# Issuing the first weight quarter from ScalarE's DMA queue instead of SyncE's

## The chip, the cores and the metric

The kernel runs on one core of one Trainium2 chip. The metric is the device time of one execution in microseconds (us); lower is better. Of the 46 executions of the kernel before, 45 lie within 0.3% of their mean (493.22 us), and the effect studied here is smaller than that, so I look at distributions and at the traces as well as at medians. A verdict of "faster" or "slower" needs 2%.

## The reference, cut to what matters

The program computes two attention blocks on the same input `x` (2048 rows of 1024) and mixes them with a gate. Only the very first stage matters here: the key projection of block A and the feature map applied to it.

```python
def _A_ref(x, wqkv, wo):
    qkv = (x @ wqkv).reshape(B, S, 3, H, Dh)...     # B=1, S=2048, D=1024, H=32
    q, k, v = qkv[0], qkv[1], qkv[2]
    phi = lambda t: jnp.where(t > 0, t + 1, jnp.exp(t)) + 1e-6
    pq, pk = phi(q), phi(k)
    ...
# then block B (sliding, dilated) and g * a + (1 - g) * b
```

## The kernel before

TensorE needs `x` transposed (`xT`) and the weights `WkA`. All loads are issued by SyncE, in program order, on one queue. `xT` comes in sixteen DMA transposes of 128 rows (256 KB each); the first half of `WkA` (512 columns) comes in four quarters of 256 KB; its second half is one 1 MB load behind the last transpose.

```python
nc.scalar.preload_act_table_set("natural_log_exp_and_others")
...
WkA = [wpool.tile([P, KT, 512], BF16, name="WkA0", tag="wa")]
nc.sync.dma_start_transpose(out=xT[:, :, 0:P], in_=rows(x, 0, P))
for i in range(4):
    if i == 2:
        nc.sync.dma_start_transpose(out=xT[:, :, P:2 * P], in_=rows(x, P, 2 * P))
    nc.sync.dma_start(out=WkA[0][:, 2 * i:2 * i + 2, :],
                      in_=A_wqkv[2 * i * P:(2 * i + 2) * P, D:D + 512].rearrange("(kt p) n -> p kt n", p=P))
for t in range(2, NB):
    nc.sync.dma_start_transpose(out=xT[:, :, t * P:(t + 1) * P], in_=rows(x, t * P, (t + 1) * P))
WkA += load_w("WkA", A_wqkv, D, "wa", only=(1,))
# ... then xrow (4 MB), WvA, WoA, WvB, WqA on the same queue
```

On TensorE, 36 small matmuls on constants come first (the warm-up), then the projection, first with the pieces of two row blocks interleaved in the order in which the loads arrive, then block by block:

```python
warm_up(36)                       # 128x128 matmuls of ones
for t, kts in ((0, (0, 1, 2, 3)), (1, (0, 1, 2, 3)), (0, (4, 5)), (1, (4, 5)), (0, (6, 7)), (1, (6, 7))):
    for kt in kts:
        project(first[t], t, kt, 0)          # quarter kt // 2 of the weights, row block t
    ...
for half in range(2):             # 16 row blocks with the first weight half, 16 with the second
    for t in range(NB):
        ...
# then G = xrow^T pk (line L202), which needs all 256 projections
```

## Time and profile before

| what | value | where it is read |
|---|---|---|
| time, median of the first 3 runs | 493.66 us (492.73 to 494.03) | the runs |
| span of the traced execution, PE busy in it | 491.1 us, 481.1 us | the page's first part |
| TensorE idle before its first real matmul | 0.68 us, until quarter one | the timeline |
| second transpose of `x` | issued 3.31, landed 7.6 us | the timeline and the line's own view |
| second weight half | issued 26.40, landed 34.87 us | the chain of waits |

The first part of the page of the kernel before gives each engine's busy time. TensorE, busy for 481.1 of 491.1 us, is the bottleneck of nearly the whole span.

```profile
PE 481.1 (98%) x3276; PEld 230.0 (47%) x3336; DVE 282.8 (58%) x548; ACT 180.6 (37%) x279; POOL 7.6 (2%) x26
```

The timeline of the kernel before, first 12 us. Columns: start, length, engine (SPq and ACTq are queue instructions, that is, the issuing of a DMA), source line, operation, destination and source, count, and in brackets the engine's idle time before and what ended it.

```profile
0.79 1.28 ACT L72 ACT_TABLE_LOAD   x1 [0.79 <-PEq L513]
0.80 1.34 SPq L97 DMA_TRANSPOSE xT<-in_A_x_dram  x1
...
1.11 4.02 PE L163 MATMUL warm<-onesb 128*128 128x128 bf16 x36 [1.11 <-DVE onesb L116]
...
2.19 1.07 SPq L101 DMA_DIRECT2D WkA_75<-in_A_wqkv_dram  x2
...
3.31 1.25 SPq L100 DMA_TRANSPOSE xT<-in_A_x_dram  x1
4.61 1.09 SPq L101 DMA_DIRECT2D WkA_75<-in_A_wqkv_dram  x2
...
5.81 1.42 PE L157 MATMUL pk_ps<-WkA_75,xT 128*128 128x512 bf16 x4 [0.68 <-DMA WkA_75<-in_A_wqkv_dram]
...
7.66 4.71 PE L157 MATMUL pk_ps<-WkA_75,xT 128*128 128x512 bf16 x20 [0.42 <-DMA xT<-in_A_x_dram]
```

SyncE needs 1.25 to 1.34 us to issue each of these two transposes and about 0.5 us to issue a quarter. TensorE waits twice, for quarter one and for the second transpose. The chain of waits of the kernel before, in the first 36 us (start, length, what), ends in SyncE's queue and the 1 MB load behind it:

```profile
25.05 1.31 SPq L104
26.35 0.04 issue
26.40 8.47 DMA WkA_96<-in_A_wqkv_dram
34.87 0.05 issue
34.92 1.25 PE pk_ps L157 x5
```

The windows view of the kernel before: window, length, busy time (count) of PE, weight loads, DVE, ACT and POOL, then clock, DMA share, GB/s. (A packet's whole time is counted in the window in which it starts, so a share can pass 1.)

```profile
1.50:2.00 0.50, 0.50 (x8) 0.50 (x6) 0.17 (x2) 0.50 (x1) 0.50 (x4) 1.00 0.00 0
2.00:2.50 0.50, 0.50 (x8) 0.50 (x6) 0.00 (x0) 0.07 (x1) 0.50 (x4) 1.00 0.09 22
2.50:3.00 0.50, 0.50 (x7) 0.50 (x6) 0.00 (x0) 0.00 (x0) 0.50 (x5) 1.00 0.99 232
3.00:3.50 0.50, 0.50 (x7) 0.50 (x6) 0.00 (x0) 0.00 (x0) 0.50 (x4) 1.00 1.17 248
3.50:4.00 0.50, 0.50 (x8) 0.50 (x6) 0.00 (x0) 0.00 (x0) 0.50 (x3) 1.00 0.85 94
4.00:4.50 0.50, 0.50 (x7) 0.50 (x6) 0.00 (x0) 0.00 (x0) 0.50 (x3) 1.00 0.72 190
```

### The profile page before, as it was taken

Reading aid. Unit: us, or ns where it says so; the run is one execution under the profiler, and the core shown is the slowest. Engines: PE = TensorE matmul, PEld = TensorE weight load, DVE = VectorE, ACT = ScalarE, POOL = GpSimd, SP = SyncE. Lnnn points to the kernel's source line nnn. Section 1 sums busy time; section 2 is a strip of 40 time slices with the busy share of each in tenths; the row PEclk is TensorE's granted clock in tenths of the full one; section 3 lists DMA queues with packets and bytes.
Section 4 is the critical chain, followed back from the end, with each engine's and each line's share of the span. In section 5 each row is a group of like instructions: output and inputs, shape, how many; then the busy total and the mean of one; then the engine's idle time right before and its main releaser. Section 6 shows DMA issues by size and latency. Waiting matters only on the chain.

```text
span 491.1 us, 8153 instructions
## 1 busy us (share of the span) xinstructions
PE 481.1 (98%) x3276; PEld 230.0 (47%) x3336; DVE 282.8 (58%) x548; ACT 180.6 (37%) x279; POOL 7.6 (2%) x26
## 2 busy tenths in 40 slices
PE   8999999999999999999999999999999999999997
PEld 5444444446444444444445444444544444444444
DVE  1666669951329999997476767676765496000000
ACT  2333321112543333332555555655565333112121
POOL 3000000000200000000000000000000000000000
PEclk9999999999999999999999999999999999999999
DMA  8999950001521222235011133111174933010101
GB/s 195 173 297 368 348 183 0 0 1 44 177 76 54 86 94 92 73 135 173 4 34 30 32 96 54 26 36 37 29 136 90 217 87 84 35 43 33 43 34 43
DMA packets 80309, 46.56 MB, mean 95 GB/s; under 512 B 53648, under 2 KB 74256, under 8 KB 80272
## 3 DMA queue, kind: packets, MB, share of 16 engines
q1 hardware_dynamic: 80272, 46.04, 34.4%
q8 instruction: 26, 0.43, 0.4%
q14 instruction: 11, 0.09, 0.1%
HBM read 21.23 MB, written 7.34 MB: 58 GB/s over the span
## 4 chain that ended last, share of the span: by engine, by line
PE 91%; SPq 5%; DMA 2%; issue 1%; DVE 0%; ACT 0%; ACTq 0%
PE kq_ps L338 23%; PE d_ps L457 21%; PE g_ps L202 11%; PE p_ps L261 11%; PE p_ps L295 8%; PE pk_ps L157 6%; SPq L104 4%; PE q_ps L295 2%; DMA WkA_96<-in_A_wqkv_dram 2%; PE kv_ps L220 1%; PE q_ps_4355 L457 1%; PE p_ps L250 1%; PE q_ps L457 1%; SPq L101 0%; PE q_ps_4236 L295 0%
## 5 line engine op out<-in xcount | busy, mean ns | idle before, releaser
L202 PE MATMUL g_ps<-pk,xrow 128*128 128x512 bf16 x251 | 55.2, 379 | 0.3
L145 DVE TENSOR_SCALAR e<-e 128x512 f32<-128x512 f32 x64 | 27.2, 425 | 42.7 <-ACT e L144 42.7
L462 ACT ACTIVATE osb<-d_ps,omg 128x512 bf16<-128x512 f32 (+1 forms) x31 | 20.9, 673 | 74.5 <-PE d_ps L457 68.7
L157 PEld LDWEIGHTS <-xT 128*128 128x128 bf16 x256 | 24.9, 98 | 32.5 <-issue 1.5
L457 PEld LDWEIGHTS <-OBT 128*128 128x128 bf16 x264 | 25.8, 98 | 29.2
L202 PEld LDWEIGHTS <-xrow 128*128 128x128 bf16 x256 | 25.0, 98 | 30.2
L261 PEld LDWEIGHTS <-xT 128*128 128x128 bf16 x256 | 25.0, 98 | 30.2
L295 PEld LDWEIGHTS <-xT 128*128 128x128 bf16 x256 | 24.2, 98 | 28.0
L144 ACT ACTIVATE e<-pk_ps 128x512 f32<-128x512 f32 x32 | 19.0, 597 | 42.3 <-PE pk_ps L157 33.2
L377 DVE TENSOR_TENSOR PT_1863<-PT_1863,mask 128x672 bf16<-128x672 bf16 (+3 forms) x42 | 23.7, 571 | 17.9 <-ACT PT_1863 L375 17.4
L338 PE MATMUL kq_ps<-xT,WqB_1846 128*128 128x512 bf16 x120 | 31.8, 379 | 1.0 <-issue 0.6
L338 PE MATMUL kq_ps<-xT,WqB_1844 128*128 128x512 bf16 x124 | 31.7, 379 | 0.7 <-issue 0.5
L377 DVE TENSOR_TENSOR PT_1864<-PT_1864,mask 128x672 bf16<-128x672 bf16 (+3 forms) x40 | 22.3, 565 | 17.0 <-ACT PT_1864 L375 16.5
L338 PE MATMUL kq_ps<-xT,WkB_1041 128*128 128x512 bf16 x122 | 31.6, 379 | 0.2
L344 DVE CAST kqt<-kq_ps 128x512 bf16<-128x512 f32 x32 | 22.0, 687 | 16.5 <-PE kq_ps L338 16.5
L338 PE MATMUL kq_ps<-xT,WkB_1039 128*128 128x512 bf16 x120 | 30.7, 379 | 0.4 <-issue 0.2
L261 PE MATMUL p_ps<-WvB_112,xT 128*128 128x512 bf16 x126 | 30.6, 379 | 0.1
L261 PE MATMUL p_ps<-WvB_110,xT 128*128 128x512 bf16 x125 | 30.6, 379 | 0.1
L266 ACT CAST tmp<-p_ps 128x512 bf16<-128x512 f32 x32 | 18.8, 588 | 30.2 <-PE p_ps L261 27.9
L457 PEld LDWEIGHTS <-pqT_4413 128*128 128x128 bf16 x200 | 19.6, 98 | 22.1
L157 PE MATMUL pk_ps<-WkA_75,xT 128*128 128x512 bf16 x125 | 28.1, 380 | 1.4 <-DMA WkA_75<-in_A_wqkv_dram 0.7
L457 PE MATMUL d_ps<-WoB_4050,OBT 128*128 128x512 bf16 (+1 forms) x126 | 28.3, 365 | 0.1
(393 smaller groups left out, 665.8 us busy)
## 6 DMA issues: line engine op xcount, KB each, us to landing
xrow<-in_A_x_dram SPq DMA_DIRECT2D x4, 1024.0 KB, 13.0
out_dram<-osb SPq DMA_DIRECT2D x31, 128.0 KB, 1.9
pqd<-tmp SPq DMA_DIRECT2D x12, 256.0 KB, 2.0
V<-tmp SPq DMA_DIRECT2D x4, 264.0 KB, 2.4
WkA_75<-in_A_wqkv_dram SPq DMA_DIRECT2D x4, 256.0 KB, 3.8
WkA_96<-in_A_wqkv_dram SPq DMA_DIRECT2D x1, 1024.0 KB, 8.5
WvA_102<-in_A_wqkv_dram SPq DMA_DIRECT2D x1, 1024.0 KB, 15.3
WvA_104<-in_A_wqkv_dram SPq DMA_DIRECT2D x1, 1024.0 KB, 14.7
```

The costliest lines, as they stand in the source:

```text
L104: nc.sync.dma_start_transpose(out=xT[:, :, t * P:(t + 1) * P], in_=rows(x, t * P, (t + 1) * P))
L144: nc.scalar.activation(out=e[:], in_=pj[:], func=ACT.Exp)
L145: nc.vector.tensor_scalar(out=e[:], in0=e[:], scalar1=1.0, scalar2=1e-6, op0=ALU.min, op1=ALU.add)
L157: nc.tensor.matmul(pj[:], lhsT=xT[:, kt, t * P:(t + 1) * P], rhs=WkA[half][:, kt, :], start=(kt == 0), stop=(kt == KT - 1))
L202: nc.tensor.matmul(pj[:], lhsT=xrow[:, t, kt * P:(kt + 1) * P], rhs=pk[:, t, half * 512:(half + 1) * 512], start=(t == 0), stop=(t == NB - 1))
L261: nc.tensor.matmul(st["pj"][:], lhsT=xT[:, kt, t * P:(t + 1) * P], rhs=WvB[half][:, kt, :], start=(kt == 0), stop=(kt == KT - 1))
L295: nc.tensor.matmul(st["pj"][:], lhsT=xT[:, kt, t * P:(t + 1) * P], rhs=WqA[half][:, kt, :], start=(kt == 0), stop=(kt == KT - 1))
L338: nc.tensor.matmul(st["pj"][:], lhsT=W[c // 4][:, kt, (c % 4) * P:(c % 4 + 1) * P], rhs=xT[:, kt, cols], start=(kt == 0), stop=(kt == KT - 1))
L344: nc.vector.tensor_copy(out=kqt[:, 1, cols], in_=st["pj"][:])
L377: nc.vector.tensor_tensor(out=ptv[:, hs], in0=ptv[:, hs], in1=m[:, None, :].broadcast_to([P, 2, W_]), op=ALU.mult)
L457: nc.tensor.matmul(st["ps"][:, 0:n], lhsT=lhsT, rhs=W[c0 // 512][:, c, c0 % 512:c0 % 512 + n], start=(side == 0 and c == 0), stop=(side == ...
L462: nc.scalar.activation(out=osb[:, 0:n], in_=st["ps"][:, 0:n], func=ACT.Copy, scale=omg[:, tb:tb + 1])
```

## The change

Quarter one need not stand behind the first transpose in SyncE's queue. ScalarE has a DMA queue too and, after its table load (0.79 to 2.07 us), nothing else to do until 10.03 us, so it issues quarter one. The other three quarters stay where they are.

```diff
-        nc.sync.dma_start(out=WkA[0][:, 2 * i:2 * i + 2, :],
-                          in_=A_wqkv[2 * i * P:(2 * i + 2) * P, D:D + 512].rearrange("(kt p) n -> p kt n", p=P))
+        (nc.sync if i else nc.scalar).dma_start(
+            out=WkA[0][:, 2 * i:2 * i + 2, :],
+            in_=A_wqkv[2 * i * P:(2 * i + 2) * P, D:D + 512].rearrange("(kt p) n -> p kt n", p=P))
```

The order of instructions on TensorE, VectorE, ScalarE and GpSimd is otherwise the same; source lines after the edit move down by one.

## The prediction

The forecast's sum is 493.66 - 0.45 = 493.2 us.

> **What bounds the kernel.** TensorE. The page's first part has PE busy 481.1 us of a 491.1 us span at a granted clock of 1.0, and PE's waits from 36 us to the end add up to under 2 us. So the change can only move the moment at which the back-to-back matmul stream begins; everything after slides by that amount. The first 35 us are not purely PE: the chain of waits runs back from the first matmul of the second half (34.92 us, waiting for WkA_96, issued at 26.40 us, 8.47 us to landing) through SyncE's queue, link after link, to its first instruction at 0.80 us. SyncE issues sixteen transposes of 1.3 us each and four weight quarters of 0.46 to 0.58 us before WkA_96.
>
> **PE's early idle time (waits, timeline).** The 36 warm-up matmuls end at 5.13 us. PE then idles 0.68 us until the first weight quarter lands (5.81; issued 2.19, so 3.6 us), later 0.42 us until the second transpose of x lands (7.65; issued 3.31, so 4.3 us), and a weight load waits 0.30 us for the third (10.22; issued 5.74, so 4.5 us). After that the matmuls need 1.73 us a row block against about 1.45 us a transpose, and PE runs without a gap until WkA_96 (0.33 us idle).
>
> **What the change does.** No matmul, byte or evacuation changes; the order is the same on all engines but for one DMA issue moved from SyncE to ScalarE, behind the table load (0.79 to 2.07 us).
> - SyncE loses one issue, 0.56 us plus 0.05 us gap: quarter two, the second and third transposes and all later issues, WkA_96 included, come about 0.6 us earlier.
> - If ScalarE's queue waits for the table load, its issue is at about 2.1 us against 2.19. [...] If the queue does not wait, quarter one lands near 4.5 us and PE starts at 5.13.
> - [...] The windows agree that little is free: DMA share 0.72 to 1.2 from 2.5 us on. So quarter one beside transpose one slows both somewhat.
>
> **Critical share.** The gates after the start are the second and third transposes; they move by at most 0.6 us, whatever quarter one does. WkA_96 must move too, or PE's gain ends in a longer wait at 34.9 us. I expect 0.45 us of the 0.6 to reach the end: 493.66 - 0.45 = 493.2 us, range 492.4 to 494.1. Chances: faster by over 2% 0.005, within 2% 0.99, slower 0.005.
>
> **What would show it.** SyncE's second transpose issued near 2.7 us instead of 3.31, landing near 7.1; WkA_96 issued near 25.8 instead of 26.40; first second-half matmul near 34.4 instead of 34.92; the span about 490.6; everything after equal in length.
>
> **What would make it wrong.** [...] transposes landing later although issued earlier; WkA_96 bound by DMA bandwidth rather than by its issue. All are below 1 us, which single runs (492.73 to 494.03) hardly resolve.

## The result

The changed kernel ran at 492.94 us median of six executions, the kernel before at 493.7 us median of six. Without the slow execution described next, the changed kernel's median is 492.80 us. The ratio is 0.9987, with a 95% interval of 0.9972 to 1.0003: the same, within 2%. A ratio here is the mean time of one kernel's fast runs over that of the other's of the same rounds, so it is not quite the ratio of the medians.

One of the six executions of the changed kernel took 2865.23 us. It happened to be the profiled one. In its trace a 512-column matmul is started every 1.32 us instead of every 0.216, six times as slow as at full speed, and already the 36 warm-up matmuls take 11.9 us instead of about 4. The clock of 1.0 reported for it says nothing: the trace holds no clock record, and the views count time without a record as full speed. VectorE and ScalarE are busy for 290.8 and 182.3 us, against 282.8 and 180.6 in the kernel before. The page of that execution reads:

```profile
PE 2859.0 (100%) x3336; PEld 751.4 (26%) x3336; DVE 290.8 (10%) x548; ACT 182.3 (6%) x279; POOL 7.6 (0%) x26
```

This never came back in the 15 other executions of the changed kernel or in any of those of the experiments. Its cause is unknown. It is left out. The profile after is therefore that of a second, normal run of the same kernel (`after_again`, 492.68 us, span 490.7). Its timeline, same columns:

```profile
0.79 1.35 SPq L97 DMA_TRANSPOSE xT<-in_A_x_dram  x1
0.79 1.28 ACT L72 ACT_TABLE_LOAD   x1 [0.79 <-PEq L514]
0.82 0.44 ACTq L101 DMA_DIRECT2D WkA<-in_A_wqkv_dram  x1
...
1.11 3.56 PE L164 MATMUL warm<-onesb 128*128 128x128 bf16 x36 [1.11 <-DVE onesb L117]
...
2.21 0.56 SPq L101 DMA_DIRECT2D WkA<-in_A_wqkv_dram  x1
...
2.81 1.24 SPq L100 DMA_TRANSPOSE xT<-in_A_x_dram  x1
4.10 1.09 SPq L101 DMA_DIRECT2D WkA<-in_A_wqkv_dram  x2
...
4.70 0.60 PE L158 MATMUL pk_ps<-WkA,xT 128*128 128x512 bf16 x2
...
5.94 0.59 PE L158 MATMUL pk_ps<-WkA,xT 128*128 128x512 bf16 x2 [0.64 <-DMA WkA<-in_A_wqkv_dram]
...
7.05 1.04 PE L158 MATMUL pk_ps<-WkA,xT 128*128 128x512 bf16 x4 [0.52 <-DMA xT<-in_A_x_dram]
```

ScalarE issued quarter one at 0.82 us, while its own table load was running: the queue did not wait. The quarter landed 2.9 us later, at 3.7 us, and TensorE went from warm-up to real work at 4.70 us with no idle time. The windows of `after_again` show the DMA engines at work earlier (first packet at 1.9 us) and without the dip at 4 us:

```profile
1.50:2.00 0.50, 0.50 (x8) 0.50 (x6) 0.17 (x2) 0.50 (x1) 0.50 (x4) 1.00 0.06 20
2.00:2.50 0.50, 0.50 (x8) 0.50 (x6) 0.00 (x0) 0.08 (x1) 0.50 (x4) 1.00 0.69 188
2.50:3.00 0.50, 0.50 (x7) 0.50 (x6) 0.00 (x0) 0.00 (x0) 0.50 (x5) 1.00 1.08 325
3.00:3.50 0.50, 0.50 (x7) 0.50 (x6) 0.00 (x0) 0.00 (x0) 0.50 (x4) 1.00 1.22 246
3.50:4.00 0.50, 0.50 (x8) 0.50 (x6) 0.00 (x0) 0.00 (x0) 0.50 (x3) 1.00 1.28 299
4.00:4.50 0.50, 0.50 (x11) 0.50 (x9) 0.00 (x0) 0.00 (x0) 0.50 (x3) 1.00 1.07 240
```

Half a microsecond times the last column, summed from 1.5 to 4.5 us, is 0.66 MB after and 0.39 MB before: by 4.5 us the engines had moved 0.27 MB more, about the quarter (0.26 MB). The chain of waits of `after_again` in the first 36 us no longer passes through the second weight half at 34 us; from 8.57 us on it is TensorE alone:

```profile
4.10 4.43 DMA WkA<-in_A_wqkv_dram
8.52 0.04 issue
8.57 1.24 PE pk_ps L158 x5
```

### The profile page after: what moved, and what is told of

Its sections match the earlier page's. It is cut to its first block, busy times and chain, and to the rows that moved or that the text cites. A ratio compares the mean times of both kernels' runs of the same rounds, so it can differ in the third digit from the quotient of the medians.

```text
span 2863.2 us, 8213 instructions
## 1 busy us (share of the span) xinstructions
PE 2859.0 (100%) x3336; PEld 751.4 (26%) x3336; DVE 290.8 (10%) x548; ACT 182.3 (6%) x279; POOL 7.6 (0%) x26
## 4 chain that ended last, share of the span: by engine, by line
PE 100%; ACT 0%; issue 0%; DVE 0%; ACTq 0%
PE kq_ps L339 24%; PE d_ps L458 22%; PE g_ps L203 12%; PE pk_ps L158 12%; PE p_ps L262 12%; PE p_ps L296 9%; PE q_ps L296 3%; PE oB L395 2%; PE s L367 2%; PE q_ps L458 1%; PE p_ps L251 1%; PE kv_ps L221 1%; PE warm L164 0%; PE z_ps L228 0%; ACT osb L463 0%
## 5 line engine op out<-in xcount | busy, mean ns | idle before, releaser
L339 PE MATMUL kq_ps<-xT,WqB 128*128 128x512 bf16 x256 | 352.9, 1672 | 0.0
L339 PE MATMUL kq_ps<-xT,WkB 128*128 128x512 bf16 x256 | 352.1, 1668 | 0.0
L262 PE MATMUL p_ps<-WvB,xT 128*128 128x512 bf16 x256 | 345.6, 1704 | 0.0
L203 PE MATMUL g_ps<-pk,xrow 128*128 128x512 bf16 x256 | 338.8, 1706 | 0.0
L158 PE MATMUL pk_ps<-WkA,xT 128*128 128x512 bf16 x256 | 338.8, 1706 | 0.0
L458 PE MATMUL d_ps<-WoA,pqT 128*128 128x512 bf16 (+1 forms) x248 | 329.1, 1664 | 0.0
L458 PE MATMUL d_ps<-WoB,OBT 128*128 128x512 bf16 (+1 forms) x248 | 329.1, 1664 | 0.0
L296 PE MATMUL p_ps<-WqA,xT 128*128 128x512 bf16 x192 | 258.6, 1708 | 0.0
L262 PEld LDWEIGHTS <-xT 128*128 128x128 bf16 x256 | 82.7, 323 | 255.4 <-issue 255.4
L158 PEld LDWEIGHTS <-xT 128*128 128x128 bf16 x256 | 82.8, 324 | 253.6 <-issue 253.6
L296 PEld LDWEIGHTS <-xT 128*128 128x128 bf16 x256 | 77.4, 306 | 235.4 <-issue 235.4
L296 PE MATMUL q_ps<-WqA,xT 128*128 128x512 bf16 x64 | 86.4, 1653 | 0.0
```

What stands on the lines that cost most here:

```text
L158: nc.tensor.matmul(pj[:], lhsT=xT[:, kt, t * P:(t + 1) * P], rhs=WkA[half][:, kt, :], start=(kt == 0), stop=(kt == KT - 1))
L203: nc.tensor.matmul(pj[:], lhsT=xrow[:, t, kt * P:(kt + 1) * P], rhs=pk[:, t, half * 512:(half + 1) * 512], start=(t == 0), stop=(t == NB - 1))
L262: nc.tensor.matmul(st["pj"][:], lhsT=xT[:, kt, t * P:(t + 1) * P], rhs=WvB[half][:, kt, :], start=(kt == 0), stop=(kt == KT - 1))
L296: nc.tensor.matmul(st["pj"][:], lhsT=xT[:, kt, t * P:(t + 1) * P], rhs=WqA[half][:, kt, :], start=(kt == 0), stop=(kt == KT - 1))
L339: nc.tensor.matmul(st["pj"][:], lhsT=W[c // 4][:, kt, (c % 4) * P:(c % 4 + 1) * P], rhs=xT[:, kt, cols], start=(kt == 0), stop=(kt == KT - 1))
L458: nc.tensor.matmul(st["ps"][:, 0:n], lhsT=lhsT, rhs=W[c0 // 512][:, c, c0 % 512:c0 % 512 + n], start=(side == 0 and c == 0), stop=(side == ...
```

## The experiments

Five theories were at stake in the end. A: SyncE's queue is shorter by one issue, so every later load comes earlier (the prediction's account). B: it is the early landing of quarter one itself that pays. C: whatever SyncE gains is given back in longer issues. H, formed after the first four runs: what differs is the moment at which TensorE goes from half to full speed. D, formed later, sharpens B: the DMA engines get work while the first transpose is still being issued, so everything queued behind lands earlier.

Two numbers read from each trace make the runs comparable. The first is g, the moment of the first weight load of the stage after the projection (the `xrow` matmuls). From g to the end of the span is 428.69 to 428.88 us in all 13 normal traces. So every difference between these kernels is made before g, in the first 65 us. The second is the landing of the second transpose. All traces in one table (us):

| run | quarter one issued | second transpose issued, landed | last half-speed matmul started | transposes' issues end | second weight half issued, landed | g |
|---|---|---|---|---|---|---|
| before | 2.19 | 3.31, 7.61 | 5.81 | 26.35 | 26.40, 34.87 | 62.34 |
| before_again | 2.21 | 3.32, 8.15 | 9.88 | 27.18 | 27.23, 34.83 | 63.37 |
| before_warm44 | 2.21 | 3.33, 7.96 | 6.43 | 26.70 | 26.75, 34.39 | 62.25 |
| after_again | 0.82 | 2.81, 7.01 | in the warm-up | 26.93 | 26.97, 33.91 | 61.89 |
| after_sample | 0.83 | 2.83, 7.23 | 6.13 | 26.65 | 26.69, 33.84 | 61.50 |
| after_warm44 | 0.82 | 2.82, 7.41 | 6.21 | 26.68 | 26.72, 33.86 | 61.87 |
| after_warm24 | 0.83 | 2.82, 7.45 | 11.73 | 27.06 | 27.11, 34.31 | 63.99 |
| after_wk1 | 0.83 | 2.82, 7.20 | in the warm-up | 30.01 | 22.89, 28.89 | 62.63 |
| sp_spare | 0.82 | 3.34, 7.25 | 4.93 | 28.08 | 28.12, 35.92 | 63.39 |
| sp_spare_warm44 | 0.83 | 3.33, 7.25 | in the warm-up | 26.50 | 26.54, 34.47 | 61.97 |
| act_late | 2.32 | 2.82, 8.16 | 9.67 | 28.14 | 28.18, 35.99 | 63.54 |
| act_late_warm56 | 2.32 | 2.83, 8.06 | in the warm-up | 26.70 | 26.75, 35.33 | 62.80 |
| act_w3 | 0.82 | 2.21, 8.94 | 12.37 | 26.96 | 27.01, 33.98 | 65.12 |

"Half speed" means a 128x512 matmul recorded at about 634 ns instead of 379, and started 427 instead of 216 ns after the one before it (start to start, read from the traces' records). Each half-speed matmul on the critical path costs 0.211 us.

### Run 1: the kernel before against itself (before_again)

No edit.

> The unchanged kernel against itself, to see how far two equal kernels differ: all theories expect a ratio of 1.000 within 0.15%. Its trace is a second sample of the first 35 us: the first second-half matmul at 34.9 us within 0.3 us, WkA_96 issued near 26.4 us.

Measured: 493.04 us median of 6 (492.71 to 495.36) against 493.08 of 11, ratio 1.0004 (0.9986 to 1.0023). So even this comparison cannot resolve 0.1%. The two traces of the same kernel differ by 1.03 us in g, more than the effect sought. Why shows in the groups by form of `before_again` in the window 6.5 to 10 us (line, engine, operation, shapes, count, busy us, mean ns):

```profile
L157 PE MATMUL pk_ps<-WkA,xT 128*128 128x512 bf16 x8 | 3.9, 615 | 0.3 <-DMA WkA<-in_A_wqkv_dram 0.2
```

A mean of 615 ns: these matmuls ran at half speed until 10.27 us, while in the first trace they ran at 379 ns from 6.13 us on. The five that come after the last wait cost 5 x 0.211 = 1.05 us. The views give the clock as 1.00 in both all the same; why is said after the runs.

### Run 2: the changed kernel again (after_again)

No edit.

> The changed kernel, for a profile in the normal state (the first one fell on an execution whose matmuls all took about six times as long). Theory A (a shorter SyncE queue makes every later load earlier): second transpose issued near 2.8 us, landing near 7.1, WkA_96 issued near 25.8, first second-half matmul near 34.4, span about 490.6, ratio about 0.999. Rival C (the transposes are paced by the DMA hardware, so an earlier issue is given back in longer issues): WkA_96 still issued at 26.4 to 26.7 us, first second-half matmul at 34.9, ratio 1.000.

Measured: 492.63 us median of 6 (492.55 to 493.14), ratio 0.999 (0.9977 to 1.0002). The second transpose was issued at 2.81 and landed at 7.01, as theory A had it, but the second weight half was issued at 26.97 us: theory C was right about that; that the DMA hardware paces the transposes, as it supposed, is not shown. SyncE's timeline of `before_again`:

```profile
5.74 21.44 SPq L104 DMA_TRANSPOSE xT<-in_A_x_dram  x14
27.23 0.58 SPq L86 DMA_DIRECT2D WkA<-in_A_wqkv_dram  x1
```

and of `after_again`:

```profile
5.23 21.69 SPq L105 DMA_TRANSPOSE xT<-in_A_x_dram  x14
26.97 0.58 SPq L86 DMA_DIRECT2D WkA<-in_A_wqkv_dram  x1
```

The fourteen transposes started 0.5 us earlier and took longer. In the table, their issues end at 26.35, 27.18 and 26.70 us with quarter one in SyncE's queue and at 26.93, 26.65 and 26.68 us in the changed kernel with 36 or 44 warm-up matmuls: no lead is left. The transpose issued after 6.5 us, for example, took 2.60 us in `after_again` and 2.07 in the first trace, and both ended near 9.1 us. Yet g is 61.89: the gain in this trace has another source than an earlier issue of the second weight half.

### Run 3: the queue as long as before, quarter one early (sp_spare)

```diff
+    spare = consts.tile([P, 2, 2], BF16, name="spare")
+    nc.sync.dma_start(out=spare[:], in_=A_wqkv[0:2 * P, D:D + 2].rearrange("(kt p) n -> p kt n", p=P))
     for i in range(4):       # quarter one still from nc.scalar
```

> The changed kernel with a spare transfer of 4 bytes a row, as many rows as the moved quarter, put back into SyncE's queue where the quarter had been. Quarter one still lands early from ScalarE's queue, but SyncE's queue is as long as before. Theory A (queue length) expects the gain gone: second transpose issued near 3.3 us, first second-half matmul near 34.9, ratio 1.000. Theory B (the early landing of quarter one is what pays) expects the gain kept: matmuls of block 0 start near 5.1 us and the second half starts as early as in the changed kernel, ratio 0.999.

Measured: 493.11 us median of 6 (492.46 to 493.83), ratio 0.9993 (0.9979 to 1.0008). The time lies between the two theories and decides nothing. The trace does: the second transpose was issued at 3.34 us, as late as before, and landed at 7.25, as early as in the changed kernel. That speaks against A. The execution was nevertheless slow (g 63.39): three transposes took 2.2 to 2.5 us to issue, TensorE waited 0.35 us for a transpose at 16 us, and the second weight half landed at 35.92 us, for which it waited 0.45 us. Long issues are not special to this trace: fourteen transposes took 20.62, 21.44, 21.69, 22.32 and 22.89 us to issue in `before`, `before_again`, `after_again`, `sp_spare` and `act_late`, where fourteen of 1.31 us with gaps of 0.04 would take 18.9.

### Run 4: the queue short, quarter one late (act_late)

```diff
+    nc.scalar.activation(out=WkA[0][:, 0, 0:2], in_=nc.const_aps.tensor(0.0, (P, 2), F32), func=ACT.Copy)
     for i in range(4):       # quarter one from nc.scalar, now waits for this write: issued at 2.32 us
```

> The changed kernel with quarter one still on ScalarE's queue but held behind a tiny ScalarE instruction that follows the table load, so that it is issued near 2.4 us, about as late as in the kernel before. SyncE's queue is short. Theory A expects the gain kept (quarter one lands near 6 us, the second transpose near 7.1 is the gate, second half starts near 34.4, ratio 0.999). Theory B expects it gone (second half at 34.9, ratio 1.000).

Measured: 494.63 us median of 6, and all six between 494.27 and 495.71; ratio 1.0032 (1.0018 to 1.0047). Neither theory had foreseen a loss of that size. The line's own view of the second transpose in `act_late` gives its issue (duration, start) and its time to landing:

```profile
L101 SPq DMA_TRANSPOSE xT<-in_A_x_dram x1: 1239/1239/1239, 2.8 to 2.8; - x1
...
DMA to landing us min/median/max: 5.3/5.3/5.3
```

Issued at 2.8 us like in the changed kernel, it landed at 8.16, as late as in the kernel before. With quarter one late, the shorter queue bought nothing. And TensorE, idle for 2.0 us before 7.16, ran seven matmuls at half speed. That led to theory H.

### Run 5: a longer warm-up before (before_warm44)

```diff
-            warm_up(36)
+            warm_up(44)
```

> The kernel before with 44 instead of 36 warm-up matmuls, so that TensorE stays busy until about 6.0 us and does not idle while it waits for quarter one (5.8 us). Theory H (what varies is the moment at which TensorE goes from half to full speed: a busy stretch interrupted at 5.13 us sometimes puts it off to about 10 us, which costs about 1 us, and the change pays by closing that gap): all executions between 492.5 and 493.4 us, none at 494 or over, matmuls of 379 ns from about 6 us on, mean as low as that of the changed kernel (0.9985 to 0.9995). Theory A (queue length) expects no change or a loss of up to 0.2 us: ratio 1.000, and executions at 494 to 495 us as before.

Measured: 492.93 us median of 5, all between 492.82 and 493.20; ratio 1.0001 (0.9989 to 1.0013) against 11 executions of the kernel before on that chip that lie between 492.40 and 494.36. The spread closed as theory H expected, but five executions are few: 3 of 12 of the kernel before took over 493.4 us on that chip, so five without one would come by chance in about one case of three. The mean (492.97) did not reach that of the changed kernel, and the ratio is missed. The groups by form of `before_warm44` in the window 6.5 to 10 us:

```profile
L157 PE MATMUL pk_ps<-WkA,xT 128*128 128x512 bf16 x13 | 3.6, 404 | 0.6 <-DMA xT<-in_A_x_dram 0.6
```

### Run 6: a shorter warm-up after (after_warm24)

```diff
-            warm_up(36)
+            warm_up(24)
```

> The changed kernel with 24 warm-up matmuls, which end near 3.7 us, a microsecond before transpose one lands. No transfer moves. Theory H expects the late release of the clock back in most executions: matmuls of about 630 ns until 8 to 11 us in the trace and a median of 493.5 to 494.5 us. Theory A expects the time of the changed kernel, 492.7 us.

Measured: 493.59 us median of 5 (493.07 to 494.67), ratio 1.0017 (1.0005 to 1.0029). No transfer moved (second transpose 2.82 to 7.45), but the same view of `after_warm24` shows half speed, and the table shows it lasting to 11.73 us:

```profile
L158 PE MATMUL pk_ps<-WkA,xT 128*128 128x512 bf16 x8 | 3.8, 625 | 0.8 <-DMA WkA<-in_A_wqkv_dram 0.7
```

The median is in theory H's range; half speed lasted a little longer than its 8 to 11 us. Theory A, which expected no change, is missed.

### Run 7: filling the hole (act_late_warm56)

`act_late` with `warm_up(56)`.

> The kernel with the held quarter on ScalarE's queue (494.6 us, 1.6 us slower than before, TensorE idle 2.0 us before 7.16 us and half speed until 10 us) with 56 warm-up matmuls that fill the idle stretch up to about 7.2 us. The quarter lands no earlier. Theory H: full speed from 6 us on, median 492.7 to 493.4 us. Rival (the late quarter and the longer SyncE queue issues themselves cost the 1.6 us): still 494.3 us or more.

Measured: 493.64 us median of 5 (493.47 to 493.93), ratio 1.0015 (1.0002 to 1.0028). The mean fell from 494.87 (`act_late`, another chip) to 493.66, with no transfer issued earlier near the start. The groups by form in the window 6.5 to 10 us, first of `act_late`:

```profile
L159 PE MATMUL pk_ps<-WkA,xT 128*128 128x512 bf16 x7 | 3.0, 606 | 2.0 <-DMA WkA<-in_A_wqkv_dram 2.0
```

then of `act_late_warm56`:

```profile
L159 PE MATMUL pk_ps<-WkA,xT 128*128 128x512 bf16 x13 | 3.1, 379 | 0.1
```

So 1.2 us of the 1.6 went with the hole and the half speed after it, or 1.0 if each is taken against the kernel before on its own chip, as theory H had it. H expected at most 493.4 and is missed by the rest: in this trace the second weight half landed only at 35.33 us and TensorE waited 0.3 us for it.

### Run 8: the whole first weight half on ScalarE's queue (act_w3)

```diff
+    nc.sync.dma_start_transpose(out=xT[:, :, P:2 * P], in_=rows(x, P, 2 * P))
+    for k0, k1 in ((0, 2), (2, 4), (4, 8)):
+        nc.scalar.dma_start(out=WkA[0][:, k0:k1, :], in_=A_wqkv[k0 * P:k1 * P, D:D + 512].rearrange("(kt p) n -> p kt n", p=P))
```

> A candidate to beat both: all of the first weight half on ScalarE's queue in three transfers (two quarters, then one half), so that SyncE issues nothing but transposes before WkA_96. Theory A: WkA_96 issued near 24.5 us, second transpose near 2.2 us, landing near 6.3, second half starts near 33 us, time 491.4 us. If the DMA engines rather than the issuing queues pace the first loads, the transposes' issues stretch, the second half starts no earlier than 34.2 us and the time stays at 492.6 us.

Measured: 494.82 us median of 6 (493.82 to 496.66), ratio 1.0041 (1.0023 to 1.0059). This is the change taken further, and it loses. Three weight transfers now run beside the first transposes: the first landed at 6.09 us instead of 4.65, the second, though issued at 2.21 us, at 8.94, and the third took 3.40 us to issue. The waits of TensorE in the first 40 us of `act_w3` (who waited for what: us in total, times, longest):

```profile
PE pk_ps L156 <- DMA xT<-in_A_x_dram: 2.0, 2, 1.0
```

After that idle time TensorE stayed at half speed until about 13 us. The second weight half was issued at 27.01 us, not at 24.5. The alternative written beside A (the DMA engines pace the first loads) was right that the transposes' issues stretch and too mild about the time; that the DMA engines pace them is not shown.

### Run 9: the changed kernel, a third trace (after_sample)

No edit.

> The changed kernel again, for a third trace and more executions, since the two kernels differ in how often an execution is slow. Theory H (the change takes away executions in which TensorE reaches full speed only near 10 us): no execution at 494 us or over, mean near 492.8 us, against a mean near 493.3 us and about one execution in six at 494 or over for the kernel before. The trace shows matmuls of 379 ns from 6 us at the latest. Theory A (a constant shift of 0.45 us): the fastest executions are also 0.4 us faster than the fastest of before (492.4 us), near 492.0 us.

Measured: 492.67 us median of 4 (492.31 to 493.08), ratio 0.9997 (0.9983 to 1.0012). No execution was slow, and the fastest was 0.09 us below the fastest of before (492.40), not 0.4. The trace has full speed from 6.48 us on rather than from 6.

### Run 10: both clocks secured (after_warm44)

The changed kernel with `warm_up(44)`.

> The changed kernel with 44 warm-up matmuls, to be set against the kernel before with 44 (492.93 us, 492.82 to 493.2). The clock is secured in both, so only the shorter SyncE queue is left between them. Theory A (the shorter queue is worth 0.45 us) expects 492.5 us. Theory H with the give-back in the transposes' issues (they end near 26.7 us in both kernels) expects 492.9 us, within 0.2 us of it.

Measured: 492.77 us median of 4 (492.16 to 493.27), mean 492.74, against 492.97 for the mean of `before_warm44` on the same chip. The difference of 0.23 us lies between what the two theories expect and inside the scatter; it is inconclusive. In the traces g is 61.87 against 62.25.

### Run 11: the second weight half earlier (after_wk1)

```diff
     for t in range(2, NB):
+        if t == NB - 3:
+            WkA += load_w("WkA", A_wqkv, D, "wa", only=(1,))
         nc.sync.dma_start_transpose(out=xT[:, :, t * P:(t + 1) * P], in_=rows(x, t * P, (t + 1) * P))
-    WkA += load_w("WkA", A_wqkv, D, "wa", only=(1,))
```

> The changed kernel with the load of the second weight half moved ahead of the last three transposes of x, so that it lands near 31 us and cannot hold the second half (it lands between 33.9 and 35.9 us in the traces so far, in the same microsecond in which TensorE gets there). If that landing is the second gate and part of the spread: no wait at the start of the second half, second half at 34.2 us or earlier, all executions below 493.0 us, median near 492.5 us. If the last transposes then come late for TensorE, a wait of up to 1 us at blocks 13 to 15 appears instead and the time is 493 us or more.

Measured: 493.52 us median of 4 (493.26 to 494.32), ratio 1.0015 (1.0002 to 1.0028). The load landed at 28.89 us and held nothing, but the transposes behind it came late, as the second alternative had it. The waits of the weight loads between 28 and 37 us in `after_wk1`:

```profile
PEld L159 <- DMA xT<-in_A_x_dram: 0.6, 1, 0.6
```

Two of the last three transposes took 2.49 and 2.61 us to issue behind the 1 MB load. Early waits were longer too in this execution (quarter three landed at 8.93 us), so not all of its g of 62.63 is due to the edit.

### Run 12: a long queue, an early quarter, a secured clock (sp_spare_warm44)

`sp_spare` with `warm_up(44)`.

> Quarter one early on ScalarE's queue, SyncE's queue kept as long as before by the spare transfer, and 44 warm-up matmuls so that the clock is secured. Over the traces so far the second transpose of x landed at 7.05 to 7.49 us wherever quarter one was issued at 0.8 us, and at 7.65 to 8.2 us wherever it was issued at 2.2 to 2.4 us, whatever the length of SyncE's queue. Theory D (the early issue pays because the DMA engines get work they can move while the first transpose is still being issued) expects the second transpose of x, issued near 3.3 us, to land at 7.1 to 7.5 us, and the time to be that of the changed kernel with 44 (492.7 us). Theory A (queue length) expects it at 7.7 to 8.2 us, and the time of the kernel before with 44 (492.9 to 493.0 us). The trace is to decide; the times are too close.

Measured: 492.48 us median of 6 (492.25 to 492.69), ratio 0.999 (0.9977 to 1.0004). The line's own view of the second transpose in `sp_spare_warm44`:

```profile
L102 SPq DMA_TRANSPOSE xT<-in_A_x_dram x1: 1242/1242/1242, 3.3 to 3.3; - x1
...
DMA to landing us min/median/max: 3.9/3.9/3.9
```

Issued at 3.33, landed at 7.25 us. Theory D's forecast of the landing holds, A's fails. In the kernel before the same issue time had given this (`before_again`, same view):

```profile
L100 SPq DMA_TRANSPOSE xT<-in_A_x_dram x1: 1239/1239/1239, 3.3 to 3.3; - x1
...
DMA to landing us min/median/max: 4.8/4.8/4.8
```

It is also the steadiest kernel, with the lowest median, but its chip differs from that of most other runs and its interval reaches above 1, so that it beats both kernels is not shown.

### What the experiments say together

The landing of the second transpose forms a two by two (`act_w3` moved more than one thing and is left out). With quarter one issued at 0.8 us it landed at 7.01 to 7.45 us (seven normal traces), with quarter one at 2.2 to 2.3 us at 7.61 to 8.16 (five), whether SyncE's queue was long or short. One trace doesn't fit: in the slow execution that was left out, quarter one was issued at 0.83 us and the second transpose landed at 7.77 us, inside the late range. What goes with the early issue is that the DMA engines get the first packets of these loads at 1.9 us instead of 2.2, are busier from 3.5 to 4 us (share 1.17 to 1.43 against 0.41 to 0.85; both hold in all 14 traces), and have quarter one out of the way when the second transpose comes. Which of these makes it land earlier the runs do not separate.

The changed kernel had 15 normal executions, 492.31 to 493.23, mean 492.79. The kernel before, counting `before_again` and each set of shared executions once, had 46, from 492.40 to 495.36, mean 493.22. The fastest are 0.09 us apart; 15 of 46 executions of before and none of 15 of the changed kernel took 493.4 us or more. If the slow ones fell at random among the 61, none among these 15 would have a chance of 0.007; but I chose that limit after seeing the times, and for the 8 of 46 at 494 us or over the chance is 0.09. In each of the three sets of rounds in which the two kernels ran side by side, the mean of the changed kernel was lower, by 0.63, 0.49 and 0.38 us. So the change probably trims slow executions rather than shifting all of them. One slow execution of before was traced (493.97 us), and there late full speed made it slow. That the other slow ones have the same cause is argued, not shown.

The traces say more about the moment of full speed than their views do. A trace's clock table (in the packed trace; no view prints it) has a record of full speed that begins where the spacing of the matmuls halves: at 4.04 us in `after_again`, 6.05 in `before`, 10.23 in `before_again`, 12.96 in `act_w3`. Earlier there is no record, and the views count that as 1.00.

Before that moment TensorE, once started, had no hole in `after_again`, one of 0.68 us in `before`, 0.75 and 0.16 us in `before_again` and two of 1.0 us in `act_w3`. `act_late`, with a hole of 2.0 us, started its last half-speed matmul at 9.67 us, `after_warm24`, with 0.8 and 0.7 us, at 11.73. Runs 6 and 7 edited the length of the warm-up alone. With 24 instead of 36 matmuls the last half-speed start moved from the warm-up (`after_again`) or 6.13 us (`after_sample`) to 11.73; with 56 instead of 36 it moved from 9.67 us into the warm-up. So in these traces full speed came later where holes came first. How much idle time makes the difference is not shown: holes of 0.68 and 0.75 us are nearly equal, and yet the two traces of the kernel before reached full speed 4.2 us apart. That no normal execution of the changed kernel reached 493.4 us would fit its full speed at 4.04 us in `after_again` and 6.48 in `after_sample`, but traces of a few executions do not show it.

Two things stay open. Which resource makes some transposes take 2 to 3 us to issue was not isolated. And the second weight half landed 6.9 to 7.2 us after its issue in the changed kernel, 7.6 to 8.5 in the kernel before, but also 7.8 to 7.9 with the spare transfer in SyncE's queue; why is not settled.

## Why the prediction was right or wrong

- **The time.** 493.2 us with a range of 492.4 to 494.1 was predicted, 492.94 measured, and "within 2%" held. That is partly luck: the range also holds the kernel before, and the 0.45 us was to come from a lead in SyncE's queue that did not last. The bound by TensorE held too: 428.7 to 428.9 us from g to the end in every trace.
- **"SyncE loses one issue ... all later issues, WkA_96 included, come about 0.6 us earlier."** This step failed. The second transpose was issued 0.5 us earlier, but the lead was gone when the transposes ended, and WkA_96 was issued at 26.7 to 27.0 us, not 25.8. The prediction had named stretched transposes among the things that would make it wrong; they did take longer (21.69 us for fourteen against 21.44 in `before_again`). And where the lead existed it was not the cause: runs 3, 4, 7 and 12 show the landing following quarter one's issue time and not SyncE's queue.
- **"The second transpose landing near 7.1."** Right (7.01 to 7.45 in the changed kernel), but not for the reason given: with the spare transfer it was issued at 3.33 or 3.34 us, as late as before, and still landed at 7.25.
- **ScalarE's issue.** Two cases are left open in the forecast; it was the second. The queue did not wait for the table load: it issued at 0.82 us. Quarter one landed at 3.7 us, earlier than the 4.5 expected, and TensorE started at 4.70 instead of 5.13, because full speed came at 4.04 us in this trace and the warm-up took 3.56 instead of 4.02 us (start at 4.93 in `after_sample`).
- **"Quarter one beside transpose one slows both somewhat."** Right for the transpose (4.65 instead of 4.2 us), wrong for quarter one, which landed in 2.9 instead of 3.6 us.
- **"DMA share 0.72 to 1.2 ... little is free."** That read the wrong stretch. What was free lay before 2.5 us, where the share was 0.09 or less, and around 4 us, where it was 0.72 to 0.85 (in `before`).
- **"0.45 us of the 0.6 to reach the end."** The means differ by 493.22 - 492.79 = 0.43 us, but not as one constant shift: the fastest executions differ by 0.09.
- **What was missing.** The prediction treated TensorE's speed as given, because the page says 1.0. In this stage the spacing of 512-column matmuls falls from 427 to 216 ns at a moment that lay between 3.9 and 13 us in the traces and that came late (9.7 us or after) in the four traces with holes of 0.75 to 2.0 us before it, and one late change costs more (1.03 us in g) than the whole change was to gain.

## What to carry to other kernels

At the start of this kernel the early issue from a second DMA queue, while the first was still issuing, went with first packets at 1.9 instead of 2.2 us and a second transpose landed at 7.01 to 7.45 instead of 7.61 to 8.16; in another kernel, check the DMA share of the first microseconds for such room, then stop, for moving more made it worse here (494.82 us). Keep TensorE busy from the warm-up into the first real matmul (filling `act_late`'s hole of 2.0 us took its mean from 494.87 to 493.66 us, on another chip), and read its speed from the spacing of matmuls, not from the clock of the views, which counts time without a record as full speed. When the gain sought is as small as the spread, find a number in the trace that carries the whole difference (g here), and compare that.
